# Operand buffers of the three-pass matmuls padded by 32 bytes, every other weight tile set 16 bytes further

## The chip, the cores and the metric

The kernel runs on one core of a Trainium2 chip, which has eight. The metric is device time in microseconds (us), the median of several runs of the whole kernel; lower is better. TensorE (PE in the profile) does the matmuls, and its weight loads are shown apart (PEld); VectorE is DVE, ScalarE is ACT, GpSimd is POOL, and SP issues most transfers.

## The reference

Attention with a causal mask and a bias from cumulated positions, then two feed-forward layers, all in float32 (2304 tokens, 512 features):

```python
scores = q @ k.T / 8 + min(-(cum[i] - cum[j]), 0)   # 32 heads, 576 x 576, causal
x = softmax(scores) @ v                             # 2304 x 512
h = x @ w_in                                        # 512 -> 2048
x = (h - tanh(h)) @ w_out                           # 2048 -> 512
out = (((x @ w1) * (x @ w2)) @ w3) @ w_o2           # 512 -> 1024, 1024 -> 1024 -> 512
```

## The kernel before

Three stages follow one another. Up to about 460 us the attention of 16 pairs of heads is interleaved, by a step table written out in the code, with the first half (8 of 16 slices) of the first feed-forward layer in blocks of 256 tokens. From 460 to 658 us the other 8 slices run in blocks of 512 tokens (the last one 256). From 660 to 700 us `w3 @ w_o2` is multiplied into one 1024 x 512 matrix. From 700 us the second layer runs as 24 units of seven products of half matrices (Strassen-Winograd), 384 tokens wide, and the results are multiplied by that matrix. The order of the matmuls is written out in the code.

Each float32 product is made of three passes on the type float32r: a value is split into a high part and the rest (`split`, L62, the second operation on the line below it), and `mm3` (L103) or `group` (L803) multiplies high by high, high by low and low by high into one PSUM sum. A tile of an operand holds its two parts behind each other. So every matmul reads two tiles in SBUF: the moving operand, 256, 384 or 512 columns of 4 bytes on each partition, and the weights, 128 columns of 4 bytes, which a weight load brings in ahead of its matmul. Nearly every matmul here has new weights, so a weight load for the next matmul lies beside each matmul.

The tiles that the change touches:

- `slot` (L59): the weights `win`, `wout` of the first layer, in 17 slots (tag `w`); two of the slots are lent to `rel` (L558) during the attention.
- `xhl`, `gh`, `gl` (L390, L436, L437, and L673, L699, L700 for the second half): the moving operands of the first layer; `xhl` also carries results out (`yo`, L421).
- `tb` (L749): the moving operands of the seven products, named `T1hl` to `T4hl`, `B11hl`, `B21hl`, `B22hl` in the profile.
- `ws` (L765): their weights, loaded from DRAM (`S`, `A` in the profile, 256 KB each), two units deep.
- `w3s` (L791): the weights of the last product; `p1`, `p2` (L876, L879): its moving operands.

An address in SBUF within 128 bytes is called a place here. The allocator puts tiles behind one another, and all of these tiles had sizes that are multiples of 512 bytes, as are all steps within a tile. So in the built program all tiles of a kind have one place: 32 for `xhl`, `gh`, `gl`, `p1`, `p2`; 96 for `win`, `wout`, `tb`, `ws`, `w3s`. The tiles `wo2` and `w3b` of the product `w3 @ w_o2` have place 32 and are not touched. So the two operands of a matmul stand 64 bytes apart in the first layer and in the last product (32 and 96), and have the same place in the seven products (96 and 96) and in `w3 @ w_o2` (32 and 32).

Of the kernel before, what the change touches and what calls it, by code (L numbers as in the profile page):

```python
# [15 lines left out]
P = 128  # L16
# [3 lines left out]
DM = 512  # L20
# [17 lines left out]
def tile_kernel(ctx: ExitStack, tc: tile.TileContext, qk, v, s, w_in, w_out, w1, w2, w3t, w_o2, outT):  # L38
# [17 lines left out]
    wf_d = dr.tile([2 * (NF - F1), P, 2, DM], F32, tag="wf_d", name="wf_d")  # L56
    wg_d = dr.tile([NG, P, 7, 2, 2 * P], F32, tag="wg_d", name="wg_d")

    def slot(name):  # L59
        return wp.tile([P, 2, DM], F32R, tag="w", name=name)  # L60

    def split(dst_hi, dst_lo, src, hi=None, lo=None):  # L62
        (hi or nc.scalar.copy)(dst_hi, src)  # L63
# [49 lines left out]
    with ExitStack() as actx:  # L113
# [266 lines left out]
        def ffn():  # L380
            pend = []
            cut = {}

            def ready(blk):
                return blk < NB and all(written[b] >= min(S, (blk + 1) * BLK - S * b) for b in range(B))

            def cut_x(blk, lo):
                xs = cut.setdefault(blk, [])
                c, c0 = len(xs), blk * BLK
                x = f2.tile([P, 2, BLK], F32R, tag="xhl", name=f"xhl{blk}_{c}", bufs=6)  # L390
                split(x[:, 0, :], x[:, 1, :], xy[:, c, c0:c0 + BLK], lo=lo)
                xs.append(x)

            for blk in range(NB):
                c0 = blk * BLK
                while not ready(blk):
                    yield False
                while len(cut.get(blk, ())) < NC:
                    cut_x(blk, nc.vector.tensor_sub)
                xs = cut[blk]  # L400
                ys = []

                def add_y(f, gh, gl, end, ys=ys, blk=blk):
                    while f not in wout:
                        next(conv)
                    if f == 0:
                        ys.extend(ps_y.tile([P, 2, BLK], F32, tag=f"y{z}", name=f"y{z}_{blk}") for z in range(2))
                    for n, (z, x) in enumerate(((0, gh), (1, gh), (0, gl))):
                        for c in range(NC):
                            o = ys[c // 2][:, c % 2, :]  # L410
                            nc.tensor.matmul(o, wout[f][:, z, P * c:P * c + P], x,  # L411
                                             start=f == 0 and n == 0 and c % 2 == 0, stop=f == F1 - 1 and n == 2,
                                             skip_group_check=True)
                            if n == 1 and c == 1:
                                yield True
                    if f == F1 - 1:
                        after[1].append(end)

                def end_y(ys=ys, blk=blk, c0=c0):
                    for z in range(2):  # L420
                        yo = f2.tile([P, 2, BLK], F32R, tag="xhl", name=f"yo{z}_{blk}", bufs=6).bitcast(F32)  # L421
                        nc.scalar.copy(yo, ys[z])
                        nc.sync.dma_start(yp_d[:, 2 * z:2 * z + 2, c0:c0 + BLK], yo)

                for f in range(F1):
                    while f not in win:
                        next(conv)
                    late = written[B - 1] == S
                    ph = ps_a.tile([P, 512], F32, tag="s", name=f"h{blk}_{f}") if late else ps_h.tile([P, 512], F32, tag="h", name=f"h{blk}_{f}")
                    hh = ph[:, :BLK]  # L430
                    for c in range(NC):
                        pace[0] = mm3(hh, win[f], P * c, xs[c][:, 0, :], xs[c][:, 1, :], c == 0, c == NC - 1)
                        if c == 1:
                            yield True
                    t = f2.tile([P, BLK], F32, tag="th", name=f"th{blk}_{f}")
                    gh = f2.tile([P, BLK], F32R, tag="gh", name=f"gh{blk}_{f}", bufs=3)  # L436
                    gl = f2.tile([P, BLK], F32R, tag="gl", name=f"gl{blk}_{f}", bufs=3)  # L437

                    def tanh(t=t, hh=hh):
                        nc.scalar.activation(t, hh, AF.Tanh)  # L440

                    def rest(t=t, hh=hh, gh=gh, gl=gl, blk=blk):
                        nc.vector.tensor_sub(t, hh, t)
                        if blk < 2:
                            split(gh, gl, t)
                        else:
                            split(gh, gl, t, hi=nc.vector.tensor_copy, lo=nc.vector.tensor_sub)

                    after[0].append(tanh)
                    after[1].append(rest)  # L450
                    yield True
                    if len(pend) > late:
                        yield from pend.pop(0)
                    pend.append(add_y(f, gh, gl, end_y))
                    if f >= 3 and ready(blk + 1) and len(cut.get(blk + 1, ())) < NC:
                        cut_x(blk + 1, nc.vector.tensor_sub)
                    if blk == NB - 1 and f:
                        next(conv2, None)
                        next(conv2, None)
                    yield True  # L460
            for p in pend:
                yield from p
            yield True
            yield True
# [200 lines left out]
    with ExitStack() as bctx:  # L665
# [4 lines left out]
        def load_split(c0, n, name):  # L670
            xs = []
            for c in range(NC):
                x = b2.tile([P, 2, 512], F32R, tag="xhl", name=f"{name}{c0}_{c}", bufs=5)  # L673
                split(x[:, 0, :n], x[:, 1, :n], xy[:, c, c0:c0 + n], lo=nc.vector.tensor_sub)
                xs.append(x)
            return xs

        def ffn_rest(step):
            for bi, (c0, n) in enumerate(blocks):
# [10 lines left out]
                for f in range(F1, NF):  # L690
                    while f not in wout:
                        next(conv2)
                    ph = ps_h.tile([P, 512], F32, tag="h", name=f"hb{c0}_{f}")
                    for c in range(NC):
                        pace[0] = mm3(ph[:, :n], win[f], P * c, xs[c][:, 0, :n], xs[c][:, 1, :n], c == 0, c == NC - 1)
                    t = b2.tile([P, 512], F32, tag="th", name=f"thb{c0}_{f}")
                    nc.scalar.activation(t[:, :n], ph[:, :n], AF.Tanh)
                    nc.vector.tensor_sub(t[:, :n], ph[:, :n], t[:, :n])
                    gh = b2.tile([P, 512], F32R, tag="gh", name=f"ghb{c0}_{f}", bufs=3)  # L699
                    gl = b2.tile([P, 512], F32R, tag="gl", name=f"glb{c0}_{f}", bufs=3)  # L700
                    split(gh[:, :n], gl[:, :n], t[:, :n], lo=nc.vector.tensor_sub)
                    if len(pend) > 1:
                        add_y(*pend.pop(0))
                    pend.append((f, gh, gl))
                    step()
# [29 lines left out]
    def operands(sb):  # L735

        c0 = 2 * T * sb
        b11, b12, b21, b22 = (xy[:, c:c + 2, c0 + T * t:c0 + T * t + T] for c in (0, 2) for t in (0, 1))
        full = {"B11": b11, "B21": b21, "B22": b22}
        out = {}  # L740
        for o in OPS:
            if o in full:
                x = full[o]
            else:
                x = r3.tile([P, 2, T], F32, tag="ts", name=f"{o}_{sb}", bufs=2)
                full[o] = x
                a, b = {"T1": (b12, b11), "T2": (b22, full["T1"]), "T3": (b22, b12), "T4": (b21, full.get("T2"))}[o]
                nc.vector.tensor_sub(x, a, b)
            w = r3.tile([P, 2, 2, T], F32R, tag="tb", name=f"{o}hl_{sb}", bufs=8)  # L749
            split(w[:, 0], w[:, 1], x, lo=nc.vector.tensor_sub if o[0] == "T" else None)  # L750
            out[o] = w
            yield out
# [6 lines left out]
    def load_unit(u):  # L759
# [2 lines left out]
        f = units[u][1]  # L762
        wts[u] = {}
        for o in WORDER:
            w = r3.tile([P, 2, 2 * P], F32R, tag="ws", name=f"{o}_{u}", bufs=14)  # L765
            nc.sync.dma_start(w.bitcast(F32), wg_d[f, :, WOP[o]])
            wts[u][o] = w

# [10 lines left out]
    for f in range(NG):  # L779
# [8 lines left out]
        ps = ps3.tile([P, 512], F32, tag=f"o{f % 2}", name=f"w3o{f}")  # L788
        for m in range(NG):
            mm3(ps, w3[:, m // 4], P * (m % 4), wo2[m][:, 0, :], wo2[m][:, 1, :], m == 0, m == NG - 1)  # L790
        o = r3.tile([P, 2, DM], F32R, tag="w3s", name=f"w3s{f}", bufs=NG)  # L791
        split(o[:, 0, :], o[:, 1, :], ps, lo=nc.vector.tensor_sub)
        w3s.append(o)
        need(0)
# [40 lines left out]
    for u, (sb, f) in enumerate(units):  # L835
# [37 lines left out]
                need(sb + 1)  # L873
        pp = temp("pp", u)
        nc.vector.tensor_mul(pp, w[:, :T], c11)  # L875
        p1 = l3.tile([P, 2, T], F32R, tag="p1", name=f"p1_{u}", bufs=3)  # L876
        split(p1[:, 0], p1[:, 1], pp, lo=nc.vector.tensor_sub)
        nc.gpsimd.tensor_mul(c12, c12, c22)  # L878
        p2 = l3.tile([P, 2, T], F32R, tag="p2", name=f"p2_{u}", bufs=NG + 1)  # L879
        split(p2[:, 0], p2[:, 1], c12)  # L880
        if prev and prev[0] == NG - 1:
            evacuate_out(os_, 2 * T * (sb - 1), f"a{sb - 1}")
# [57 lines left out]
```

## Time and profile before

| | us |
|---|---|
| three runs | 987.78, 989.79, 992.14 |
| median | 989.79 |
| the profiled execution's own time | 990.76 |
| its span, first to last instruction | 988.6 |
| TensorE busy | 947.5 (96%) |
| weight loads busy (beside the matmuls) | 813.1 (82%) |
| VectorE, ScalarE, GpSimd busy | 566.2, 418.6, 253.5 |

A matmul's own duration in the profile covers its way through the array, which overlaps the next one's; what a stream of matmuls costs is the distance from one start to the next. That distance is called the pitch here. It is read where a view gives the length of an unbroken run of matmuls and their count, or the starts of two groups.

### The profile page before, as it was taken

The page shows a single profiled execution, that of the slowest core. Times are in us where ns is not written, and L with a number is a line of the kernel's source. Part 1 is how long each engine was busy: PE and PEld are TensorE (multiplying, and loading weights), DVE is VectorE, ACT ScalarE, POOL GpSimd, SP SyncE. Part 2 cuts the span into 40 slices and gives each one's busy share as a digit, 9 for nine tenths or more (in the row PEclk, how much of TensorE's full clock was granted, in tenths as well). Part 3 has the DMA queues.
Part 4 walks back from the last instruction along what each step waited for, and adds up shares of the span by engine and source line. Part 5 has one row for each costly group of instructions (what it writes and reads, how often), then busy time and mean ns, then how long its engine had stood idle before and what let it go on. Part 6 is the DMA issues. An engine that isn't in the chain of part 4 may idle for free.

```text
span 988.6 us, 16314 instructions
## 1 busy us (share of the span) xinstructions
PE 947.5 (96%) x5950; PEld 813.1 (82%) x5953; DVE 566.2 (57%) x1311; ACT 418.6 (42%) x1029; POOL 253.5 (26%) x254
## 2 busy tenths in 40 slices
PE   6878899999999999999999999989999999999997
PEld 3455677778787888998888888878899999999997
DVE  7885757555666664776886766686422712251221
ACT  2564578876666654333433333332322402231221
POOL 3332566863333330000000000012312502250220
PEclk9978899999999999999999999999999999999999
DMA  6656657442233311389664545265266636664621
GB/s 191 213 191 219 239 162 267 168 139 76 97 108 113 104 30 35 111 292 399 237 229 159 213 143 198 86 234 203 88 202 200 189 123 199 193 193 134 193 68 64
DMA packets 67711, 165.66 MB, mean 168 GB/s; under 512 B 7504, under 2 KB 22000, under 8 KB 65584
## 3 DMA queue, kind: packets, MB, share of 16 engines
q1 hardware_dynamic: 63312, 148.89, 44.9%
q10 hardware_dynamic: 4320, 15.73, 4.9%
q8 instruction: 47, 0.77, 0.3%
q14 instruction: 32, 0.26, 0.1%
HBM read 127.74 MB, written 36.86 MB: 166 GB/s over the span
## 4 chain that ended last, share of the span: by engine, by line
PE 77%; DVE 7%; DMA 6%; POOL 4%; issue 3%; ACT 2%; ACTq 0%; SPq 0%; POOLq 0%; DVEq 0%
PE W L806 10%; PE hb L107 9%; PE yb L107 9%; PE h L107 8%; PE y L411 8%; PE o L822 5%; PE Y L806 5%; PE q L822 5%; PE w3o L107 5%; PE pv L307 3%; PE s_B L210 3%; POOL pr L189 2%; PE V L806 2%; PE pt_B L281 2%; DMA wf_d<-park_win 1%
## 5 line engine op out<-in xcount | busy, mean ns | idle before, releaser
L107 PEld LDWEIGHTS h<-xhl,win 128*128 128x128 f32 x864 | 108.2, 192 | 21.2 <-issue 12.1
L107 PE MATMUL h<-xhl,win 128*128 128x256 f32 x864 | 123.0, 289 | 0.8 <-DVE xhl L64 0.6
L107 PE MATMUL hb<-x,win 128*128 128x512 f32 (+1 forms) x480 | 106.7, 372 | 0.0
L107 PE MATMUL yb<-ghb,wout 128*128 128x512 f32 (+1 forms) x320 | 97.4, 372 | 1.1 <-ACT ghb L63 1.1
L107 PEld LDWEIGHTS hb<-x,win 128*128 128x128 f32 x480 | 83.6, 188 | 17.4
L189 POOL TENSOR_SCALAR pr<-cb,cq 128x384 f32<-128x384 f32 (+1 forms) x48 | 86.4, 1815 | 10.5 <-PE pt_B L281 10.5
L411 PE MATMUL y<-gh,wout 128*128 128x256 f32 x576 | 87.6, 292 | 0.0
L64 POOL TENSOR_TENSOR B11hl<-xy,B11hl 128x768 fp32r<-128x768 f32 x3 | 5.6, 1852 | 310.7 <-DMA S<-wg_d 307.9
L270 ACT ACTIVATE pr<-pr,nm 128x128 f32<-128x128 f32 (+2 forms) x120 | 71.3, 595 | 19.2 <-DVE nm L248 19.0
L411 PEld LDWEIGHTS y<-gh,wout 128*128 128x128 f32 x576 | 74.4, 193 | 5.7 <-issue 4.3
L210 PE MATMUL s_B<-qk 64*96 64x512 f32 (+2 forms) x256 | 60.2, 524 | 13.4 <-ACT pr L266 8.4
L878 POOL TENSOR_TENSOR c<-c,c 128x384 f32<-128x384 f32 x24 | 25.8, 1076 | 172.5 <-DVE c L862 172.5
L107 PEld LDWEIGHTS yb<-ghb,wout 128*128 128x128 f32 x320 | 58.2, 188 | 12.8 <-ACT ghb L63 1.3
L822 PE MATMUL o<-p,w3s 128*128 128x384 f32 x288 | 61.2, 335 | 1.0 <-ACT p L63 1.0
L107 PE MATMUL yb<-glb,wout 128*128 128x512 f32 (+1 forms) x160 | 59.3, 373 | 0.5 <-DVE glb L64 0.5
L248 DVE CUSTOM_DVE_ANT_0 pr<-s_B,pr 96x512 f32<-96x512 f32 (+1 forms) x72 | 44.6, 640 | 21.8 <-PE s_B L210 21.8
L281 PE MATMUL pt_B<-ident,pr 96*128 96x96 f32 (+1 forms) x384 | 53.1, 262 | 1.0 <-DVE cq L582 1.0
L822 PEld LDWEIGHTS o<-p,w3s 128*128 128x128 f32 x288 | 50.5, 188 | 1.4 <-ACT p L63 1.3
L822 PE MATMUL q<-p,w3s 128*128 128x384 f32 x288 | 51.0, 336 | 0.1
L822 PEld LDWEIGHTS q<-p,w3s 128*128 128x128 f32 x288 | 50.0, 188 | 0.4 <-DVE pp L875 0.4
L290 ACT COPY pf_B<-pt_B 128x512 f32<-128x512 f32 (+2 forms) x72 | 35.9, 499 | 31.4 <-PE pt_B L281 27.6
L107 PE MATMUL w3o<-wo,w3b 128*128 128x512 f32 x192 | 45.6, 400 | 2.7 <-DVE xy L709 2.7
(169 smaller groups left out, 1878.4 us busy)
## 6 DMA issues: line engine op xcount, KB each, us to landing
S<-wg_d SPq DMA_DIRECT2D x96, 256.0 KB
A<-wg_d SPq DMA_DIRECT2D x72, 256.0 KB
qk<-in_qk SPq DMA_DIRECT2D x16, 576.0 KB
raw_w<-in_w SPq DMA_DIRECT2D x16, 512.0 KB
wg_d<-pks SPq DMA_DIRECT2D x8, 1024.0 KB
raw_w<-in_w3t SPq DMA_DIRECT2D x16, 512.0 KB
raw_win<-in_w_in ACTq DMA_DIRECT2D x15, 512.0 KB
raw_wout<-in_w_out ACTq DMA_DIRECT2D x15, 512.0 KB
```

What stands on the lines that cost most here:

```text
L107: i = nc.tensor.matmul(ps, a, b, start=first and n == 0, stop=last and n == 2, skip_group_check=skip)
L189: nc.gpsimd.tensor_scalar(out=t[:pw, e, :w], in0=p.cb[:pw, e, :w], scalar1=c, scalar2=0.0, op0=ALU.add, op1=ALU.min)
L210: latest[0] = nc.tensor.matmul(ps[e][:PW[i], o:o + k1 - k0], x[:, 0, CH0[i]:CH0[i] + PW[i]], x[:, 1, k0:k1], start=(i, k0, k1, o) == UNITS ...
L248: nc.vector.tensor_tensor_reduce(out=t[:pw, k0:k1], in0=ps[:pw, o:o + k1 - k0], in1=t[:pw, k0:k1], scale=-0.125, scalar=nm[:pw, 5:6] if k0 ...
L270: nc.scalar.activation(t[:pw, :], t[:pw, :], AF.Exp, bias=m, scale=-1.0, accum_out=p.sums[:pw, e, c:c + 1])
L281: nc.tensor.transpose(pt[:, at:at + pw], p.pr[i][:pw, e, KC0[kj]:KC0[kj] + P], ident[:pw, :pw])
L290: (nc.vector.tensor_copy if j == "B2" and not p.first else nc.scalar.copy)(pf[:, :at], pt[:, :at])
L307: nc.tensor.matmul(p.pv[D * e:D * e + D, c:p.nq], p.vs[:, e, kj], pf[:, beg:end], start=z == 0, stop=z == len(todo) - 1, skip_group_check= ...
L411: nc.tensor.matmul(o, wout[f][:, z, P * c:P * c + P], x, start=f == 0 and n == 0 and c % 2 == 0, stop=f == F1 - 1 and n == 2, skip_group_c ...
L806: nc.tensor.matmul(ps[:, :T], w[:, x, P * j:P * j + P], b[:, y, j], start=first and j == n == 0, stop=last and j == 1 and n == 2, skip_gro ...
L822: nc.tensor.matmul(os_[c][:, :T], w3s[f][:, a, P * c:P * c + P], p[:, b], start=f == 0 and n == 0, stop=f == NG - 1 and n == 2, skip_group ...
L878: nc.gpsimd.tensor_mul(c12, c12, c22)
```

## The change

A helper `apart` makes every tile of the list above 8 elements (32 bytes) longer on each partition and uses all but those bytes. So the buffers of a pool stand at steps of a multiple of 128 plus 32 bytes, and their places go round 0, 32, 64, 96. For weights (`slot`, `ws`, `w3s`) every other tile begins 16 bytes into its buffer (`half`); the 32 bytes of padding lie half in front and half behind there. `slot` counts its tiles for that, the others go by the parity of the slice `f`.

No instruction is added, removed or moved: the instructions of each engine stand in the same order before and after, with the same shapes. In the built program the moving operand's place differs from that of the matmul ahead at 1129 of the 4464 float32r matmuls of lines 107, 411, 806 and 822, and at 146 before. The distance of the two operands' places, 64 or 0 before, is spread over 0, 16, 32 to 112, each for some 400 to 770 matmuls. Two subtractions on GpSimd, of `B21hl` and `B22hl` at the end of the third stage, wait for one transfer queue more than before, since the new buffers overlap further slots of the first layer by some bytes; on the other engines only one cast takes such a wait over from another.

```diff
+    def apart(pool, parts, n, tag, name, bufs=None, half=False):
+
+        kw = {} if bufs is None else {"bufs": bufs}
+        t = pool.tile([P, parts * n + 8], F32R, tag=tag, name=name, **kw)
+        o = 4 if half else 0
+        t = t[:, o:o + parts * n]
+        return t.rearrange("p (a b) -> p a b", a=parts) if parts > 1 else t
+
+    slots = [0]
+
     def slot(name):
-        return wp.tile([P, 2, DM], F32R, tag="w", name=name)
+        slots[0] += 1
+        return apart(wp, 2, DM, "w", name, half=slots[0] % 2 == 0)
...
-                x = f2.tile([P, 2, BLK], F32R, tag="xhl", name=f"xhl{blk}_{c}", bufs=6)
+                x = apart(f2, 2, BLK, "xhl", f"xhl{blk}_{c}", 6)
...
-                    gh = f2.tile([P, BLK], F32R, tag="gh", name=f"gh{blk}_{f}", bufs=3)
-                    gl = f2.tile([P, BLK], F32R, tag="gl", name=f"gl{blk}_{f}", bufs=3)
+                    gh = apart(f2, 1, BLK, "gh", f"gh{blk}_{f}", 3)
+                    gl = apart(f2, 1, BLK, "gl", f"gl{blk}_{f}", 3)
...
-                x = b2.tile([P, 2, 512], F32R, tag="xhl", name=f"{name}{c0}_{c}", bufs=5)
+                x = apart(b2, 2, 512, "xhl", f"{name}{c0}_{c}", 5)
...
-            w = r3.tile([P, 2, 2, T], F32R, tag="tb", name=f"{o}hl_{sb}", bufs=8)
+            w = apart(r3, 2, 2 * T, "tb", f"{o}hl_{sb}", 8).rearrange("p a (b t) -> p a b t", b=2)
...
-            w = r3.tile([P, 2, 2 * P], F32R, tag="ws", name=f"{o}_{u}", bufs=14)
+            w = apart(r3, 2, 2 * P, "ws", f"{o}_{u}", 14, f % 2 == 1)
...
-        o = r3.tile([P, 2, DM], F32R, tag="w3s", name=f"w3s{f}", bufs=NG)
+        o = apart(r3, 2, DM, "w3s", f"w3s{f}", NG, f % 2 == 1)
...
-        p1 = l3.tile([P, 2, T], F32R, tag="p1", name=f"p1_{u}", bufs=3)
+        p1 = apart(l3, 2, T, "p1", f"p1_{u}", 3)
...
-        p2 = l3.tile([P, 2, T], F32R, tag="p2", name=f"p2_{u}", bufs=NG + 1)
+        p2 = apart(l3, 2, T, "p2", f"p2_{u}", NG + 1)
```

## Rows read from the trace of the kernel before

**Rows 1.** The page: busy time and share of the span by engine.

```profile
PE 947.5 (96%) x5950; PEld 813.1 (82%) x5953; DVE 566.2 (57%) x1311; ACT 418.6 (42%) x1029; POOL 253.5 (26%) x254
```

**Rows 2.** Three stretches, all engines: granted TensorE clock, DMA share, GB/s last.

```profile
60.00:380.00 320.00, 307.12 (x2369) 239.54 (x2367) 199.95 (x636) 206.17 (x591) 149.19 (x156) 0.97 0.42 142
460.00:632.00 172.00, 172.00 (x742) 138.69 (x741) 122.97 (x212) 62.53 (x105) 0.00 (x0) 1.00 0.53 193
700.00:975.00 275.00, 272.45 (x1554) 269.75 (x1553) 90.04 (x144) 71.38 (x145) 67.74 (x56) 1.00 0.53 156
```

**Rows 3.** Matmuls grouped by line and shape: count | busy, mean ns | idle before.

```profile
L107 PE MATMUL h<-xhl,win 128*128 128x256 f32 x864 | 123.0, 289 | 0.8 <-DVE xhl L64 0.6
L107 PE MATMUL hb<-x,win 128*128 128x512 f32 x384 | 94.6, 396 | 0.0
L411 PE MATMUL y<-gh,wout 128*128 128x256 f32 x576 | 87.6, 292 | 0.0
L107 PE MATMUL yb<-ghb,wout 128*128 128x512 f32 x256 | 85.2, 395 | 0.0
L822 PE MATMUL o<-p,w3s 128*128 128x384 f32 x288 | 61.2, 335 | 1.0 <-ACT p L63 1.0
L822 PE MATMUL q<-p,w3s 128*128 128x384 f32 x288 | 51.0, 336 | 0.1
L107 PE MATMUL yb<-glb,wout 128*128 128x512 f32 x128 | 50.6, 396 | 0.0
L411 PE MATMUL y<-gl,wout 128*128 128x256 f32 x288 | 45.5, 281 | 1.4 <-POOL gl L64 1.4
...
L806 PE MATMUL Y<-B22hl,S 128*128 128x384 f32 x144 | 28.8, 334 | 0.0
```

**Rows 4.** The chain that ended last, unbroken runs: start, length in us, count.

```profile
454.93 7.69 PE hb L107 x33
...
675.12 32.66 PE w3o L107 x144
790.99 16.64 PE q L822 x96
```

**Rows 5.** The same chain, within 394 to 447 us.

```profile
401.20 1.36 PE y L411 x12
402.56 1.36 PE h L107 x12
```

**Rows 6.** The timeline from 12.6 us, TensorE: start, length, group.

```profile
12.65 1.24 PE L196 MATMUL spare<-zeros,identb 128*128 128x512 bf16 x5
```

**Rows 7.** One tile's instructions: those matmuls (ns min/median/max, first and last start).

```profile
L196 PE MATMUL spare<-zeros,identb x41: 377/379/634, 2.3 to 39.5; 128*128 128x512 bf16 x41
```

**Rows 8.** The timeline from 806 us, TensorE: starts of the groups of one unit.

```profile
807.46 1.21 PE L806 MATMUL W<-B11hl,A 128*128 128x384 f32 x6
808.51 1.20 PE L806 MATMUL V<-B21hl,A 128*128 128x384 f32 x6
809.55 0.85 PE L822 MATMUL o<-p,w3s 128*128 128x384 f32 x4
810.24 1.21 PE L806 MATMUL W<-T2hl,S 128*128 128x384 f32 x6
811.29 1.20 PE L806 MATMUL Y<-B22hl,S 128*128 128x384 f32 x6
812.33 0.85 PE L822 MATMUL o<-p,w3s 128*128 128x384 f32 x4
...
816.85 1.20 PE L806 MATMUL W<-B11hl,A 128*128 128x384 f32 x6
```

**Rows 9.** The timeline from 300 us and from 398 us, TensorE.

```profile
300.98 0.64 PE L411 MATMUL y<-gl,wout 128*128 128x256 f32 x4
301.45 0.44 PE L281 MATMUL pt_B<-ident,pr 128*128 128x128 f32 x3
...
399.22 0.62 PE L411 MATMUL y<-gl,wout 128*128 128x256 f32 x4
399.67 1.52 PE L107 MATMUL h<-xhl,win 128*128 128x256 f32 x12
```

**Rows 10.** Who TensorE waited for, 700 to 975 us: in total, times, longest.

```profile
PE W L806 <- ACT s L843: 1.4, 1, 1.4
PE o L822 <- ACT p L63: 1.0, 1, 1.0
```

More of the change, by code (lines that the diff above doesn't have):

```diff
@@ L420, in end_y @@
                     for z in range(2):
-                        yo = f2.tile([P, 2, BLK], F32R, tag="xhl", name=f"yo{z}_{blk}", bufs=6).bitcast(F32)
+                        yo = apart(f2, 2, BLK, "xhl", f"yo{z}_{blk}", 6).bitcast(F32)
                         nc.scalar.copy(yo, ys[z])
@@ L698, in ffn_rest @@
                     nc.vector.tensor_sub(t[:, :n], ph[:, :n], t[:, :n])
-                    gh = b2.tile([P, 512], F32R, tag="gh", name=f"ghb{c0}_{f}", bufs=3)
-                    gl = b2.tile([P, 512], F32R, tag="gl", name=f"glb{c0}_{f}", bufs=3)
+                    gh = apart(b2, 1, 512, "gh", f"ghb{c0}_{f}", 3)
+                    gl = apart(b2, 1, 512, "gl", f"glb{c0}_{f}", 3)
                     split(gh[:, :n], gl[:, :n], t[:, :n], lo=nc.vector.tensor_sub)
```

## The prediction

> **What bounds the kernel now.** I read the page first: TensorE is busy for 96% of the span, weight loads for 82%, the next engine for 57% [rows 1]. The second view, three stretches, tells where there is room: from 460 to 632 us TensorE has no gap at all, from 700 to 975 us it is busy for 272.45 of 275.00 us, and only in the attention, 60 to 380 us, is it idle for 13 of 320 us; the granted clock is 1.00 in the two late stretches and 0.97 in the attention [rows 2]. In the last stage TensorE waits for others twice, 2.4 us together, both times for ScalarE [rows 10]. So the pitch of the matmuls is the time, nearly one to one after 460 us.
>
> The pitch is read from unbroken runs. 33 matmuls with 512 columns take 7.69 us, 233.0 ns each; the 144 of `w3o`, also 512 columns, take 32.66 us, 226.8 ns each; 96 matmuls with 384 columns take 16.64 us, 173.3 ns [rows 4]; 12 with 256 columns take 1.36 us, 113.3 ns [rows 5]. For comparison, five bf16 matmuls with 512 columns stand in 1.24 us [rows 6], each lasting 0.379 us by itself [rows 7], so that four pitches are 0.861 us, 215 ns each. Scaled by columns that would be 161 ns at 384 and 108 ns at 256. The float32r matmuls thus take 18.0 ns (512 columns, operands 64 bytes apart), 11.8 ns (512, same place), 11.9 ns (384) and 5.7 ns (256) more than bf16's rate. This excess is what a change of places can reach. That bf16 has none at 1.00 clock does not say that places cause it: it moves half the bytes, and its weights are half as long too.
>
> **The change.** It adds no instruction. What it removes is the common place of all tiles of a kind; what it adds is a change of place at 983 more matmuls (1129 for 146). Its effect is a sum over three classes of touched matmuls, counted from the groups [rows 3]: 256 columns, 864 + 576 + 288 of the attention stage, and 192 of the last block, 1920; 512 columns, 384 + 256 + 128 = 768; 384 columns, 288 + 288 and seven products of 144, 1584. The 192 of `w3o` keep their places.
>
> *Steady pitch with other distances.* The trace has two distances, 64 and 0. At 512 columns 0 is better, by 233.0 - 226.8 = 6.2 ns. At 384 columns they are equal: `q` (64 apart) has 173.3 ns [rows 4], and V, a product (0 apart), has six from 808.51 to 809.55 us, 173.3 ns [rows 8]. At 256 columns only 64 occurs. Distances of 16, 32 and 48 do not occur, and no row prices them. From below, they could take the whole excess away: 1920 x 5.7 = 10.9 us, 1584 x 11.9 = 18.8 us, 768 x 18.0 = 13.8 us, 43.5 us together; from above, nothing shows a loss in the steady state beyond what follows for 256 columns. Between these ends I take what the two known distances show as a spread: half of 6.2 ns at 512 columns, 768 x 3.1 = -2.4 us, and nothing at 384 and 256.
>
> *Each change of place.* The last stage shows this wait already, since it goes from `o` (moving operand at 32) to a product (at 96) and back three times in a unit. One unit lasts from 807.46 to 816.85 us, 9.39 us; its 54 matmuls at 173.3 ns would take 9.36 us [rows 8]. So six changes cost 0.03 us, 5 ns each. By groups: the six of `W<-T2hl` behind an `o` take 811.29 - 810.24 = 1.05 us, 10 ns more than the six of V; the four of `o` take 0.69 us, no more than four at 173.3 ns. 983 x 5 ns = +4.9 us. The bounds are the two directions by themselves: 0, and 983 x 10 ns = +9.8 us.
>
> *What else moves.* A weight tile that begins 16 bytes later is filled by the same transfers. In the last stage they take 0.53 of the transfer engines' time [rows 2], and no wait of TensorE ends on one [rows 10]; the cover is the buffers for a second unit, one unit being 9.39 us. Writes of VectorE, ScalarE and GpSimd to padded tiles keep their shapes; these engines are at 57%, 42% and 26% [rows 1], and if a write took longer it would first eat their idle time. The waits that GpSimd takes over are for transfers into the first layer's slots, hundreds of us old by then. All at 0.
>
> *Sum.* +4.9 - 2.4 = +2.5 us on the profiled execution's 990.76, 993.3 us. That execution stands 0.97 us above the median of 989.79, so the forecast is 992.3 us, rounded to **992 us**: +0.25%, within the 0.5% (4.9 us) that a measurement of this kernel can tell from no change.
>
> **A rule beside the trace.** The row first: with the next weights loading beside it, a float32r matmul is 11.8 to 18.0 ns behind bf16's rate at 512 columns [rows 4, 6, 7], and its pitch shifts when its operand's place does [rows 8]. The Trainium skill, "TensorE: Matmul & The Clock Gate", section "What happens when you issue a matmul", says that the moving operand and the weights come through two independent read ports, so that loading weights takes nothing from the running matmul. By that rule the places would change nothing, and the sum would be 0, 989.8 us. The page "SBUF — State Buffer", section "Door 1: The DMA port swizzle", speaks of lines of 16 bytes, each crossing to a new one being paid; the new places are all multiples of 16, so no operand would touch more lines than before, which also gives 0. The trace disagrees with the first in that something does slow float32r, and no run here shows lines.
>
> **Rivals.**
>
> *The standing collision goes (faster).* If weights and moving operand collide because they have run at distances 64 and 0 throughout, the other distances would be freer. For it: an excess at every width, and 6.2 ns between the two distances at 512. Against: at 384 columns 0 and 64 give the same to 0.1 ns, as if the distance did not count. A quarter to a half of the 43.5 us is 11 to 22 us; taking a third, 14 us, with no cost of changes: 990.76 - 14.5 - 0.97 = 975 us.
>
> *A second, worse rhythm (slower).* The same matmuls at the same places run at two pitches: four of `y<-gl` take 301.45 - 300.98 = 0.47 us, 117.5 ns, and four others 399.67 - 399.22 = 0.45 us, 112.5 ns [rows 9]. So places alone do not settle the pitch; how a run is entered does, and long runs with one place settle into the better one. The change breaks runs after every three matmuls in `h` and `hb`, where each of the four `xhl` tiles has its own place. If no run settles any more, 1920 x 4.5 ns = 8.6 us at 256 columns, and the 10 ns of a bad change at the 467 further changes that fall to 384 and 512 columns (516 of the 983 fall to 256), 4.7 us: +13.3 us, 1003 us. It decides from 7.6 ns per change on, where 983 x 7.6 - 2.4 = +5 us.
>
> *It does nothing.* The excess belongs to reading 4 bytes per column at the full clock, wherever they are: 989.8 us. For it: equal pitch at 384. Against: the 10 ns behind each `o`. Both pages' rules lead here.
>
> *Transfers to odd places become slow.* They would have to go from 0.53 to nearly 1.00 of their engines' time in the last stage before TensorE waits. Half the weight tiles move, so those would have to take nearly three times as long. Then some us per unit late; 1000 us or more.
>
> **How the numbers follow.** Forecast (small re-settling, 987 to 997 us): 0.32. Nothing depends on places (988 to 992): 0.12. Collision goes: 0.30. Worse rhythm: 0.22. Transfers: 0.04. The likeliest is the forecast, 992 us. Faster by over 0.5% (below 984.8): the collision case and a little of the forecast's lower bound, 0.31. Slower (above 994.7): worse rhythm, transfers, and a sixth of the forecast, 0.31. Within: 0.38. The range must reach both other cases: from 974, just past a third of the excess, to 1003, the worse rhythm as priced.
>
> **What the profile after would show.** Unbroken runs in the chain give the pitch again. Step one is right if 512 columns of the second stage come to about 230 ns on average, and 384 columns to 173 in runs of one place; a fall to 165 ns or below at 384 would prove the collision case. Step two is right if the groups of a unit take 1.05 us where their place changes and a unit about 9.41 us for 9.39 (78 of the further changes fall to the 24 units, three each). The rival rhythm would show as 117 ns in the 256-column runs between 394 and 447 us, where 113.3 stands now [rows 5]. Waits of TensorE on `S` or `A` transfers would show the last rival. The forecast fails above all if distances of 16, 32 or 48 bytes, which no row prices, have a pitch of their own.

## The result, and the profile after

The changed kernel takes 995.87 us (median of 9 runs, 992.87 to 998.80) where the kernel before takes 990.04 (9 runs, 986.54 to 992.14). The ratio is 1.0063, 95% interval 1.0044 to 1.0082: slower by 5.8 us. That is inside the range of the forecast and 3.6 us above the sum of 992.3 us; it is also above 994.7 us, in the slower band that the prediction gave 0.31. The profiled execution has a span of 994.8 us, 6.2 more than before.

The page of the changed kernel, first line, beside [rows 1]: TensorE is busy 3.8 us longer and its weight loads 6.4 us; the other engines stay within 1 us.

```profile
PE 951.3 (96%) x5953; PEld 819.5 (82%) x5953; DVE 567.1 (57%) x1311; ACT 418.6 (42%) x1029; POOL 253.5 (25%) x254
```

The chain that ended last, unbroken runs (start, length, count), beside [rows 4], and runs of 256 columns beside [rows 5]:

```profile
407.18 1.43 PE y L422 x12
408.60 1.41 PE h L118 x12
410.01 1.41 PE y L422 x12
...
462.01 7.68 PE hb L118 x33
...
679.32 32.74 PE w3o L118 x144
...
795.67 16.78 PE q L833 x96
```

The starts tell in which stage the time goes. `hb` begins at 462.01 where it began at 454.93: +7.1 us in the attention stage. At `w3o` the lead is 4.2 us, at `q` 4.7, at the end 6.2. The lengths tell the pitch: 12 matmuls with 256 columns take 1.41 to 1.43 us, 117.5 to 119.2 ns each, where [rows 5] has 113.3; 96 with 384 columns take 16.78 us, 174.8 ns for 173.3; 33 with 512 columns take 7.68 us, as before in this run, while the mean over all of them is 1.2 ns lower (table below); `w3o`, whose operands were not touched, takes 32.74 for 32.66.

The timeline of TensorE in the last stage, one unit and the group behind `o`, beside [rows 8]:

```profile
812.29 1.22 PE L817 MATMUL W<-B11hl,A 128*128 128x384 f32 x6
813.34 1.20 PE L817 MATMUL V<-B21hl,A 128*128 128x384 f32 x6
814.38 0.86 PE L833 MATMUL o<-p,w3s 128*128 128x384 f32 x4
815.08 1.22 PE L817 MATMUL W<-T2hl,S 128*128 128x384 f32 x6
816.14 1.21 PE L817 MATMUL Y<-B22hl,S 128*128 128x384 f32 x6
...
821.76 1.22 PE L817 MATMUL W<-B11hl,A 128*128 128x384 f32 x6
```

A unit takes 821.76 - 812.29 = 9.47 us for 9.39, so 24 units some 1.9 us more. The stretches of [rows 2] and the waits of [rows 10] again:

```profile
60.00:380.00 320.00, 304.90 (x2323) 237.99 (x2321) 199.43 (x629) 204.04 (x586) 149.05 (x156) 0.97 0.41 142
460.00:632.00 172.00, 172.00 (x748) 139.47 (x747) 121.39 (x208) 64.62 (x109) 0.00 (x0) 1.00 0.57 208
PE W L817 <- ACT s L854: 1.4, 1, 1.4
PE o L833 <- ACT p L74: 0.9, 1, 0.9
```

TensorE still has no gap from 460 to 632 us, waits for ScalarE twice in the last stage and for no transfer. Between 60 and 380 us it is busy 2.2 us less than before at the same granted clock: its waits within the attention grew. The longest of them, up to 460 us, for ScalarE's `pr`, after (first) and before (second; in total, times, longest):

```profile
PE s_B L221 <- ACT pr L277: 11.3, 2, 8.1
```

```profile
PE s_B L210 <- ACT pr L266: 8.4, 2, 6.7
```

A part of the loss is hidden in this execution. Behind its wait ahead of `w3o` (2.68 us idle) the kernel before ran at a granted clock of 0.58 for 4 us, near the lower level of 1.2 GHz; the changed kernel, after 2.43 us idle, stayed at 1.00, which is 2.4 GHz. PE alone from 660 to 664 us, before (first) and after (second):

```profile
660.00:664.00 4.00, 4.00 (x12) 0.58 1.05 399
```

```profile
660.00:664.00 4.00, 1.96 (x12) 1.00 0.79 269
```

At 0.42 below full clock, 4 us are some 1.7 us. That is more than half of the 2.9 us by which the lead shrinks between `hb` and `w3o`; the better pitch at 512 columns gave 0.9 us.

All means below are distances from the start of one matmul to the start of the next, taken from one trace of each kernel at the granted clock of 1.00, where TensorE did not wait. The sum is what the three differences would make, by 1920, 1584 and 768 matmuls. Beside it stands the measured difference to the kernel before, run beside it: first that of the medians, then the ratio, which is not that of the medians and can tell up to 1.4 us more or less (`best`: 0.9940 would be -5.9 us).

```
             256 col   384 col   512 col   sum us   measured us   ratio (95%)
before        114.8     173.8     233.3
after         118.3     175.0     232.1     +7.7       +5.8       1.0063 (1.0044-1.0082)
e_moving      118.1     174.9     231.8     +6.9       +4.0       1.0044 (1.0020-1.0067)
e_weights     118.2     175.1     232.5     +8.0       +5.7       1.0055 (1.0033-1.0077)
d0_256        118.8     173.8     233.3     +7.7       +6.7       1.0066 (1.0044-1.0089)
d0_512        115.5     173.8     226.7     -3.7       -5.1       0.9948 (0.9930-0.9967)
best          115.4     173.4     226.7     -4.6       -4.5       0.9940 (0.9916-0.9963)
d192_512      114.8     173.7     228.9     -3.5       -2.7       0.9981 (0.9965-0.9996)
best2         115.8     173.4     226.8     -3.7       -4.2       0.9943 (0.9921-0.9965)
```

The sums lie within the intervals of the times, or (`e_moving`, `e_weights`, `d192_512`) within half a microsecond of them.

### The profile page after: what moved, and what is told of

Read it like the earlier page. It is cut to its first block, busy times and chain, and to the rows that moved or that the text cites. A ratio compares the mean times of both kernels' runs of the same rounds, so it can differ in the third digit from the quotient of the medians.

```text
span 994.8 us, 16318 instructions
## 1 busy us (share of the span) xinstructions
PE 951.3 (96%) x5953; PEld 819.5 (82%) x5953; DVE 567.1 (57%) x1311; ACT 418.6 (42%) x1029; POOL 253.5 (25%) x254
## 4 chain that ended last, share of the span: by engine, by line
PE 82%; DMA 7%; DVE 5%; ACT 2%; issue 2%; POOL 1%; SPq 0%; ACTq 0%; POOLq 0%; DVEq 0%
PE W L817 10%; PE hb L118 9%; PE yb L118 9%; PE y L422 9%; PE h L118 9%; PE o L833 5%; PE Y L817 5%; PE q L833 5%; PE w3o L118 4%; PE pv L318 4%; PE s_B L221 4%; PE pt_B L292 3%; PE V L817 2%; PE s_A L221 1%; PE pt_A L292 1%
## 5 line engine op out<-in xcount | busy, mean ns | idle before, releaser
L422 PE MATMUL y<-gh,wout 128*128 128x256 f32 x576 | 90.1, 296 | 0.0
L422 PEld LDWEIGHTS y<-gh,wout 128*128 128x128 f32 x576 | 76.4, 195 | 5.5 <-issue 4.6
L212 POOL TENSOR_SCALAR_AFFINE_SELECT pr<-pr 128x256 f32<-128x256 f32 (+2 forms) x60 | 23.8, 411 | 94.3 <-issue 73.0
```

The lines of the kernel that those rows point to most:

```text
L422: nc.tensor.matmul(o, wout[f][:, z, P * c:P * c + P], x, start=f == 0 and n == 0 and c % 2 == 0, stop=f == F1 - 1 and n == 2, skip_group_c ...
```

## The experiments

**Theory A:** each change of place costs, so the spread of the moving operand's places is at fault. **Theory B:** each pair of places has a pitch of its own in the steady state, and the change only gave up good pairs. The first expectations word B by the distance of the two places; Theory D, in later ones, is B with the way in which a run is entered added.

**m1_places: 64 pairs by themselves.** Matmuls alone, 24 in a row for each pair of places and each width.

```diff
+    for n in (512, 384, 256):
+        for m in range(8):
+            for w in range(8):
+                o = bank()
+                for i in range(24):
+                    mm(o, n, m, w, i == 0, i == 23)
```

> Leaves the whole computation out: it only runs float32r matmuls with new weights each, 24 in a row, for each of 8 places of the moving operand and 8 of the weights (steps of 16 bytes), at 512, 384 and 256 columns; the output is filler. If the cost lies in changes of place (theory A), each run settles after some ten matmuls and the settled pitch is the same for all 64 pairs within 1%: 113.3 or 117.5 ns at 256, 173.3 at 384, 227 to 233 at 512 columns. If it lies in the distance of the two places (theory B), distances of 16, 32 and 48 settle 3 ns or more above distance 64 at 256 columns, where the changed kernel has 118.3 ns for 114.8. If it lies in the moving operand's place alone (theory C), the rows of one moving place are alike and differ from the others by 3 ns or more.

The timeline of TensorE in this kernel (`mc` is the moving tile at place 64, `wb`, `wc`, `wd` weights at 32, 64, 96):

```profile
106.83 5.76 PE L50 MATMUL o<-mc,wb 128*128 128x512 f32 x24
112.43 5.61 PE L50 MATMUL o<-mc,wc 128*128 128x512 f32 x24
117.88 5.75 PE L50 MATMUL o<-mc,wd 128*128 128x512 f32 x24
```

From start to start, 24 at 64/32 take 5.60 us, 233.3 ns each, and 24 at 64/64 take 5.45 us, 227.1. Means of the last 12 over all pairs:

```
columns   lowest (pairs there)   highest   mean of 64   at (32,96), the pair before
512         226.7  (10)            236.7      231.5        233.3
384         173.3  (27)            180.0      175.0        174.8
256         113.3  ( 6)            120.4      118.2        117.8
```

So pairs do have pitches of their own, and the changed kernel's means, 232.1, 175.0 and 118.3, lie within 0.6 ns of those over all pairs. The distance alone does not settle them, as the expectation had it: with the same place for both, 512 columns have 226.7 at (32,32) and 233.3 at (16,16). The kernel before had a poor pair for 512 columns and, at 256, a rhythm near the lowest. But no distance is the good one at all widths: with the same multiple of 32 for both, 512 columns have the lowest pitch, 226.7, and 256 columns nearly the highest, 120.0. One pair, (80,16), has the lowest at both, 226.7 and 113.3, and 176.7 at 384; m3_entries below has the same three numbers, and no kernel here uses it.

**m2_changes: what a change costs by itself, and how a run is entered.** The same tiles; runs of 96 with the place fixed or changed, and runs of 24 behind a bf16 matmul of 256 to 286 columns.

```diff
+        for pm, pw in (((1,), (3,)), ((1, 1, 1, 2, 2, 2, 3, 3, 3, 0, 0, 0), (3,)), ((1, 2, 3, 0), (3,)),
+                       ((1,), (3,) * 12 + (7,) * 12), ((1,), (3, 7)), ((1, 3), (3,))):
+            o = bank()
+            for i in range(96):
+                mm(o, n, pm[i % len(pm)], pw[i % len(pw)], i == 0, i == 95)
```

> Leaves the whole computation out, as the kernel of the table of places does. First 16 runs of 24 float32r matmuls at places 32 and 96, each entered behind a bf16 matmul that is 2 columns longer than the last; then runs of 96 with the places changed in six ways: never, moving place by 32 bytes every three matmuls, by 32 at each, weights' place by 16 bytes every twelve, at each, moving place by 64 at each. Theory A (changes cost): at 256 columns the 16 entries end in two pitches, 113.3 and 117.5 ns, at the same places; with a moving place that changes every three, the pitch is 116 to 118 ns at 256 and 175 at 384 columns for 113.3 and 173.3 without changes; the weights' place costs less than 1 ns per matmul. Theory B (distance): each run has the mean of the settled pitches of its distances, and the weights' changes cost as much as the moving operand's. All 16 entries then end in one pitch.

In ns, last 72 of 96, moving place fixed / changed every three / at each matmul: 233.3 / 233.3 / 232.5 at 512 columns, 173.3 / 175.6 / 175.0 at 384, 113.3 / 118.3 / 118.3 at 256. For the moving operand, a fee for each change would have made "at each" three times as dear as "every three", and it is not. These mixes of places lie within 2 ns of the means of their four pairs in m1_places, 231.9, 173.7 and 118.2. Not every mix is a mean: moving by 64 to and fro at each matmul gave 226.7 at 512, where its two pairs have 233.3 and 226.7; and weights whose place changed every twelve / at each had 232.2 / 230.7 at 512, 175.2 / 173.3 at 384, but 115.0 / 118.3 at 256, so fast changes can cost something at that width. All 16 entries at 256 columns settled at 113.3, where m1_places had 117.8 at the same pair: what ran ahead matters too.

**e_moving and e_weights: one half of the change each.**

```diff
-        t = pool.tile([P, parts * n + 8], F32R, tag=tag, name=name, **kw)
-        o = 4 if half else 0
+        pad = 0 if tag in ("w", "ws", "w3s") else 8
+        t = pool.tile([P, parts * n + pad], F32R, tag=tag, name=name, **kw)
+        o = 0
```

`e_weights` has `8 if ... else 0` instead and keeps the 16 bytes.

> The change's padding for the moving operands alone (xhl, gh, gl, tb, p1, p2); weights keep their size and one place. 1130 matmuls change the moving place, as in the change. Theory A: most of the change's cost, +4 to +6 us against the kernel before, with 117 to 118 ns at 256 columns. Theory B: distances here are 0, 32, 64 and 96 only; if the 16-byte ones are the dear ones, +1 to +3 us.

> The change's padding and the 16 bytes for the weights alone (w, ws, w3s); every moving operand has place 32, in the seven products too, so no matmul changes the moving place. Theory A: -1 to +1 us against the kernel before, with 113 to 115 ns at 256 columns and a unit of 9.36 us where it was 9.39. Theory B: all eight distances occur as in the change, so +4 to +6 us with 118 ns at 256 columns.

Runs of 96 `q` in the chain of `e_moving` (first line, 175.1 ns a matmul) and `e_weights` (second, 174.3 ns):

```profile
796.11 16.81 PE q L834 x96
```

```profile
796.13 16.73 PE q L834 x96
```

`e_moving` by itself came out as A had it (+4.0 us; B had expected +1 to +3). `e_weights` tells the two apart: with the weights alone spread, no moving operand changes its place any more often than before, and the kernel loses as much (+5.7 us) as with the whole change. So A falls for the moving operand. Nor do the halves add up. Both follow from B: spreading one operand already goes through good and bad pairs alike, and two spreads reach no worse mean than one.

The weights do change their place 491 times in `e_weights`, for 4 before, but the trace shows that this is not what costs. Its 256-column matmuls, sorted by the addresses in the built program, from the fourth of a run at one pair on (m1_places' names; mean ns):

```
pair            (32,96)   (32,80)   (32,32)   (32,16)
e_weights         114.0     118.1     119.4     119.7
m1_places         117.8     118.1     120.0     120.1
```

The old pair, (32,96), keeps its good rhythm amid the spread, and the other pairs have the pitch that they have by themselves.

**m3_entries: the table again behind bf16, and fewer weight columns.** Before each run stands a bf16 matmul of 128 columns; nine runs more have 64 and 32 weight columns.

```diff
+                bf(128)
                 o = bank()
...
+            for p in (P, 64, 32):
```

> Leaves the whole computation out: the table of 64 pairs of places again, but with each run of 24 entered behind one bf16 matmul of 128 columns; then three pairs with weights of 128, 64 and 32 columns. Theory D (a pair of places and the way of entry set a lasting rhythm, and the change spreads good pairs to the mean of all): the means over the 64 pairs come out as in the first table within 0.5 ns (118.0 at 256, 175.0 at 384, 231.3 at 512), though single pairs move; 32 and 96 at 256 columns goes from 117.8 to 113.3. Whatever is read with the weights: if the excess over bf16's rate comes from the weight load beside the matmul, it falls with the weights' columns, at 512 from 12 to 18 ns to under 6 with 32 columns; if it comes from reading 4-byte columns alone, it stays.

The means came back: 231.4, 175.0 and 117.9, with 163 of 192 runs within 1 ns. But (32,96) at 256 columns stayed at 117.8, not 113.3. The same run of 24, behind the same bf16 matmul, came again later in this kernel and then had 113.3, so the matmul just ahead does not choose the rhythm. The two runs in the timeline:

```profile
712.46 3.10 PE L50 MATMUL o<-mb,wd 128*128 128x256 f32 x24
...
972.33 3.00 PE L50 MATMUL o<-mb,wd 128*128 128x256 f32 x24
```

And a shorter weight load did not help: at 512 columns and (32,96) 233.3, 232.8 and 231.7 ns with 128, 64 and 32 weight columns, while a load itself lasted 188, 134 and 108 ns. A collision as long as the load would have shrunk with it. At (32,32) the pitch even rose, 226.7, 230.0 and 231.7, so the weights' columns do count, only not by the length of the load.

**d0_256 and d0_512: a constant pair, moved by 64 bytes.** The kernel before with 64 bytes ahead of the buffers of the attention stage's 256-column matmuls (first diff; its second line keeps the attention's own tiles behind them at their place, 128 bytes further), or of the second stage's (second). Both operands then have place 96; nothing varies.

```diff
+        f2.tile([P, 16], F32, tag="gap", name="gap", bufs=1)
...
+        a2.tile([P, 16], F32, tag="gap", name="gapa", bufs=1)
```

```diff
+        b2.tile([P, 16], F32, tag="gap", name="gapb", bufs=1)
```

> The kernel before with xhl, gh and gl of the attention stage moved by 64 bytes: both operands at place 96 throughout, no change of place added. Theory D: the first table has 120.0 ns for this pair at 256 columns and the kernel before 114.8, so up to 1728 x 5.2 = 9 us, some of it in the attention's idle time: +6 to +9 us. Theory A (only changes of place cost): -1 to +1 us.

> The kernel before with the moving operands of the second stage moved by 64 bytes: both operands at place 96 for the 768 matmuls of 512 columns and the 192 of 256 there. Theory D: 226.7 ns for 233.3 at 512 columns, -5.1 us, and some 5 to 6 ns more at 256, +1.1 us: -3 to -5 us in all. Theory A: -1 to +1 us.

The timeline of TensorE in `d0_256`, and the chain of `d0_512`:

```profile
404.11 1.60 PE L107 MATMUL h<-xhl,win 128*128 128x256 f32 x12
405.55 1.12 PE L413 MATMUL y<-gh,wout 128*128 128x256 f32 x8
```

```profile
452.15 7.48 PE hb L107 x33
```

12 matmuls of `d0_256` stand in 405.55 - 404.11 = 1.44 us, 120.0 ns, and the kernel loses 6.7 us without one change of place more than before. 33 of `d0_512` take 7.48 us, 226.7 ns each for 233.0, and the kernel wins 5.1 us, as much as the 768 x 6.6 ns that the places of 512 columns were worth; the 192 matmuls of its last block, at 119.9 ns for 113.6, should have taken 1.2 us of that back, and the sum in the table has it. The micro runs had both pitches, 120.0 and 226.7.

**best: each width at its best pair known by then.** `d0_512`, with `p1`, `p2` moved by 64 bytes and the 256-column block at the end of the second stage 64 bytes further into its buffers (shown for `xhl`; the same for `gh`, `gl`).

```diff
+                x = x[:, :, 16:16 + n] if n < 512 else x
...
+    l3.tile([P, 16], F32, tag="gap", name="gapl", bufs=1)
```

> As the kernel with distance 0 in the second stage, but the last block of 256 tokens uses its buffers from 64 bytes on, so that it keeps places 32 and 96, and p1, p2 of the last stage go to place 96, so that no matmul there changes its moving place. Theory D: -5.1 us in the second stage and 24 units x 0.03 us = -0.7 us in the last: -5 to -6.5 us against the kernel before. Theory A: only the last stage's changes count: -0.7 us.

It is faster than both kernels, 0.9940 to the one before, and cannot be told from `d0_512`. The last stage is where it should be: a unit has 9.36 us, as the starts in its timeline show, and nothing is lost behind an `o`, since `o` no longer has another place.

```profile
812.03 1.20 PE L811 MATMUL W<-B11hl,A 128*128 128x384 f32 x6
...
814.80 1.20 PE L811 MATMUL W<-T2hl,S 128*128 128x384 f32 x6
815.84 1.20 PE L811 MATMUL Y<-B22hl,S 128*128 128x384 f32 x6
...
821.39 1.20 PE L811 MATMUL W<-B11hl,A 128*128 128x384 f32 x6
```

The 256-column block at the end of the second stage missed: 117.8 ns, not 113.3.

**m4_kinds: how far up the address counts, and what the excess belongs to.**

```diff
+            for k in (0, 1, 2, 4, 8):
+                run(n, mv[m][:, 32 * k:32 * k + n], wt[w])
+            for k in (1, 2, 4):
+                run(n, mv[m][:, :n], wt[w][:, 32 * k:])
...
+            run(n, mb[m][:, :2 * n:2], wb[w])
```

> Matmuls alone, the kernel's own computation left out: runs of 24 behind a bf16 matmul of 128 columns, mean distance of the last 12, at four pairs of places (moving, weights): (32,96), (32,32), (96,96), (0,32). Three questions. First, whether a place within 128 bytes is all that counts of an address: the moving operand is read 128, 256, 512 and 1024 bytes further into its tile, then the weights 128, 256 and 512 bytes further. If it is all, each of these runs lies within 1 ns of the one it is moved from (three in four, since single pairs move by chance); if higher address bits decide too, they spread as the 64 pairs did, 226.7 to 236.7 ns at 512 columns, 173.3 to 180 at 384, 113.3 to 120.4 at 256. Second, whether the weights must change: with one weight tile again and again the excess over bf16's 216 ns at 512 columns goes if it comes from new weights, and stays at 10 ns or more if it comes from reading the moving operand. Third, whether it belongs to the type or to the bytes: plain bf16 should have 216, 162 and 108 ns at every pair; bf16 read with a step of 4 bytes covers as many bytes as float32r does: about 216 ns if the type makes the excess, 226 or more if the 4 bytes for each column do.

The pairs keep their names within 128 bytes. The timeline at the pair (32,32), 512 columns: the moving operand as it is, 128 and 256 bytes further, then the weights 128 bytes further:

```profile
59.06 5.85 PE L61 MATMUL o<-mb,wb 128*128 128x512 f32 x24
...
64.97 5.71 PE L61 MATMUL o<-mb,wb 128*128 128x512 f32 x24
...
70.74 5.84 PE L61 MATMUL o<-mb,wb 128*128 128x512 f32 x24
...
88.46 5.74 PE L61 MATMUL o<-mb,wb 128*128 128x512 f32 x24
```

128 bytes further is another pitch (226.7 ns for 232.9), 256 bytes further is the old one, and moving the weights by 128 does what moving the other operand does. At 512 and 384 columns moving either operand by 128 bytes gave the same pitch to 0.1 ns at each of the four pairs, and 256, 512 or 1024 bytes stay within 0.8 ns of the unmoved pair. (At 256 columns the pair (32,96) goes to and fro between 113.3 and 117.8 ns.) So what counts is the address within 256 bytes, not within 128. There the two operands stood at 160 and 32 in the first of these rows and both at the same address in the second and fourth; the pair of the kernel before, as built, is (160, 224). The old names hide this: (32,96) is (160,224) in m1_places, where 512 columns have 233.3 ns, and (160,96) in this run, where they have 228.9.

In the same run, with one weight tile again and again: 228.9, 232.9, 232.8 and 233.3 ns at the four pairs, against 228.9, 232.9, 232.6 and 233.3 with new weights each time. That does not take the load away: the trace has a load beside each of those matmuls too.

```profile
200.56 5.36 PEld L61 LDWEIGHTS o<-mb,wd 128*128 128x128 f32 x24
```

Plain bf16 has 215.8 ns everywhere at 512 columns. Bf16 read with a step of 4 bytes has 225.0 to 226.7, as these rows show (first plain, then with the step):

```profile
229.55 5.34 PE L61 MATMUL o<-mxb,wxb 128*128 128x512 bf16 x24
...
251.38 5.56 PE L61 MATMUL o<-mxb,wxb 128*128 128x512 bf16 x24
```

So at 512 columns the step of 4 bytes alone costs bf16 9 to 11 ns, about what float32r has above bf16's rate at its best pair (226.7); the 6.6 ns on top hang on the two addresses. At 256 columns the step brings bf16 from 109.2 to 113.3, again float32r's lowest. At 384 it does not reach that far: 168.9 to 170.0 for 162.5, where float32r's lowest is 173.3. The sizes agree at two widths and not at the third, so that the 4 bytes for each column make all of the excess, whatever the type, is not shown.

**d192_512 and best2: the address within 256 bytes, in the kernel.** `d192_512` moves the second stage's buffers by 128 bytes, so that the place within 128 stays what it was (first diff, to the kernel before). `best2` moves the last block of `best` by 128 bytes (second, to `best`; the same for `gh`, `gl`).

```diff
+        b2.tile([P, 32], F32, tag="gap", name="gapb", bufs=1)
```

```diff
-                x = x[:, :, 16:16 + n] if n < 512 else x
+                x = x[:, :, 48:48 + n] if n < 512 else x
```

> The kernel before with one edit: the moving buffers of the second stage stand 128 bytes further, so the place within 128 bytes is what it was (32, weights 96), and only the address within 256 changes (160 before, now 32, weights at 224). If the place within 128 bytes is all, the 512-column pitch stays at 233.3 ns and the time is that of before. If the address within 256 bytes decides, the matmuls alone had 228.9 ns at such a pair where they had 233.3 at the one of before: 768 x 4.4 ns = 3.4 us less, of which the last block gives back 192 x 4.5 ns = 0.9 us if its 256-column matmuls go from 113.3 to 117.8 ns, as they did in the best version so far, which had them at these places: ratio about 0.9975, pitch in the second stage 228.9.

> The best version so far with the operands of the last 256-column block 128 bytes further, so that they stand at 160 and 224 within 256 bytes, as in the kernel before, where it had put them at 32 and 224. If the address within 256 bytes decides, the 192 matmuls of that block run at 113.3 ns instead of 117.8, 0.9 us less than the best version: ratio about 0.993 to the kernel before. If it was how the block is entered, they stay at 117.8 and the ratio at 0.994. The pitch tells the two apart; the times are too near to each other.

The chain of `d192_512` at the start of the second stage, and its timeline in the last block:

```profile
456.29 7.57 PE hb L107 x33
...
643.70 1.52 PE L107 MATMUL hb<-x,win 128*128 128x256 f32 x12
645.06 0.28 PE L107 MATMUL yb<-ghb,wout 128*128 128x256 f32 x1
```

The 512-column matmuls run at 7.57 / 33 = 229.4 ns (mean 228.9), at an unchanged place within 128 bytes, and the ratio is 0.9981. That was as expected. At 256 columns both expectations failed. (32, 224) has 1.36 / 12 = 113.3 ns here and had 117.8 in `best`; (160, 224) has a mean of 113.6 in the block of the kernel before and 117.7 in `best2`. So at these pairs 256 columns have two rhythms. That what ran ahead decides between them is likely, since the last block's addresses within 256 bytes are the same; no run shows what it is. `best2` is no better than `best`.

## Why the prediction was right, and where its sum was not

**What bounds the kernel.** Right. The time followed the pitch, within 3 us, in every run; no wait of TensorE for a transfer appeared in any of them.

**Steady pitch with other distances.** This term was mis-sized, in sign too, and by the table it is the whole effect. The prediction took -2.4 us at 512 columns and nothing at 384 and 256, because the trace has two distances and 384 columns had one pitch at both. Measured: -0.9 us at 512 (1.2 ns of the 3.1 taken), +1.9 us at 384, +6.7 us at 256. The pitch at 256 columns, 113.3 ns, was already the lowest that any pair shows, so a spread could only lose there; [rows 5] had no second distance that would have told. The sentence on distances that no row prices named this way of failing.

**Each change of place.** The reading of [rows 8] holds: with `p1`, `p2` at the place of the other tiles the 10 ns behind each `o` are gone. Carrying them to 983 other changes does not: `e_weights` has none of these and loses as much, and in m2_changes a change at each matmul costs no more than one in three. The +4.9 us came near the measured +5.8 for a wrong reason: a unit, which this step would have left at 9.41 us, has 9.47. That the range held the time is luck as far as these two terms go, -2.4 and +4.9 us where the runs show +7.7 and no further cost.

**What else moves: nothing.** Right for the transfers and the other engines. The attention's own waits took some of the +7.1 us of that stage, beside 1728 x 3.5 ns = 6.0 us by the pitch.

**The rivals.** The slower one had the symptom, 117 ns in the 256-column runs, and not the cause: runs need not be broken for it, since `d0_256` has 120 ns with its runs as before, and in `e_weights` the old pair stays at 114.0. What it said of two rhythms at one pair holds, and how much of the loss in the runs that are broken every three is theirs stays open. A gain by other places is there at 512 columns alone and with the pair chosen, not spread: -5 us, where the whole gap to bf16's rate had been 13.8; that a collision went is not shown. That nothing depends on places falls, by `d0_256` and `d0_512`. The Trainium skill, "TensorE: Matmul & The Clock Gate", section "What happens when you issue a matmul", has the weights come through a read port of their own, so that loading them takes nothing from the running matmul. The traces do not bear that out here: the weights' address alone shifts the pitch by 6.2 ns (232.9 to 226.7 in m4_kinds), and fewer weight columns shift it by 5.0 (226.7 to 231.7 in m3_entries).

**Open.** Why the two addresses matter, when the pitch does not follow the length of the weight load and new weights do not matter, and what chooses the rhythm at 256 columns, these runs do not show. No run leaves the load out. The sums of `e_moving` and `e_weights` stay 2 to 3 us above their times.

## What to carry to other kernels

Where TensorE has no gaps, look at the distance from start to start in an unbroken run for each width, and compare widths with a bf16 run: an excess that differs between equal widths was a matter of addresses here. Spreading buffers over all places gave about the mean of the good and the bad ones; measure the pairs in a kernel of matmuls alone and give each width a constant pair, which was worth 0.5% here. A row that prices one case says little of a thousand others until an experiment has separated what varies together.

## What the runs showed of the hardware

- The pitch of float32r matmuls depends on the addresses of both operands within 256 bytes: 226.7 to 236.7 ns at 512 columns, 173.3 to 180.0 at 384, 113.3 to 120.4 at 256.
- Widths want different pairs: both operands at the same multiple of 32 within 256 bytes is best at 512 (226.7) and bad at 256 (120.0). (80,16) is lowest at both (226.7, 113.3), but not at 384 (176.7).
- Reading with a step of 4 bytes costs bf16 9 to 11 ns at 512 columns (225.0 to 226.7 for 215.8), 6 to 8 at 384 (168.9 to 170.0 for 162.5), 4 at 256 (113.3 for 109.2).
- 256 columns have two rhythms, 113.3 and 117.8 ns, at the same pair of addresses behind the same matmul (m3_entries).
